# Hashed attention and a SiLU layer on one core: batch 0's second product in seven block products, shifted weight loads, and score products over all 128 rows

## The chip, the core and the metric

The kernel runs on one core of a Trainium2 chip. The core's engines run side by side, each through its own list of instructions in order: TensorE (PE in the profile; its weight loads are shown as PEld), VectorE (DVE), ScalarE (ACT), GpSimd (POOL) and SyncE (SP), which here only issues transfers. Transfers run on 16 DMA engines that all queues share. The metric is the device time of one execution in microseconds (us); the time before is the median of 11 runs, 300.68 us.

## The reference

Four batches of eight heads, 768 positions, head width 64. Queries and keys are hashed to six sign bits by a projection; a score counts only where all six bits of query and key agree. The attention output, 3072 tokens of width 512, goes through a layer with 2048 hidden units.

```python
q_bits = (einsum('bhsd,dk->bhsk', q, proj) > 0)
k_bits = (einsum('bhsd,dk->bhsk', k, proj) > 0)
mask   = (q_bucket[:, :, :, None] == k_bucket[:, :, None, :])
scores = where(mask, (1/8) * q @ k.T, -1e9)
attn   = softmax(scores)
x      = (attn @ v) rearranged to 3072 tokens x 512
h      = x @ w_in                      # 512 x 2048
out    = (h * sigmoid(h)) @ w_out      # 2048 x 512
```

## The kernel before

**Attention.** Heads go in pairs; pair p holds heads 2p and 2p+1 and there are 16 pairs, four to a batch. For each pair there is a tile `QKA` (even head) and a tile `QKB` (odd head), each 128 rows by 1536 columns of f16: q in the first 768 columns, k in the last. Four slots of each are used in turn (`p % NSL`). In `QKA` rows 0 to 63 hold the scaled head and the rows from 64 on hold the mask bits (six bits and a constant row), so that one product gives score plus mask; rows above 70 are not defined. In `QKB` rows 64 to 127 hold the head, the bits stand from row 0 on, and the rest of rows 0 to 63 was set to zero at the start (L159).

The work is cut into 288 units, nine to a head. Unit w has three parts: `score(w)` (L371), one or two matmuls with 512 columns in all into a PSUM tile `s_ps`, followed by ScalarE's exponential into `u`; and `av(w)` (L392), four matmuls of `u` with the values into `o_ps`. `score` runs three units ahead (`LEAD = 3`): loop turn w issues `av(w)` and then `score(w+3)`. The `s_ps` tiles have the tag "s" with three PSUM buffers, and the output tiles `o2_ps` of the hidden layer's second product have the same tag: while an output tile is open, the scores share the buffers that are left. Which buffer a tile gets is fixed when the program is built.

**How a pair gets ready.** Pairs from 6 on: `load_blocks(p)` (L86) brings q and k as eight transfers of 96 KB with 128-byte rows, issued by SP. `block_unit` (L252) transposes them on VectorE into `qk32`. `cast_unit` (L260, GpSimd) fills the head's rows. `proj_unit` (L282) multiplies `qk32` of two pairs with the projection on TensorE into two PSUM tiles of the tag "m" and VectorE makes bits of them. `bits_unit` (L334) puts the bits into `QKA` and `QKB`: by VectorE copies for pairs up to 7, and by eight small transfers on SP for each two pairs above 7 (L343).

**The hidden layer.** For each batch, `mm1` multiplies `w_in` with the transposed attention output `xT`, for 512 of the batch's tokens (ci 0, here called f) and for the other 256 (ci 1, here s), into `h_ps` (tag "m", three buffers). ScalarE takes the hyperbolic tangent and VectorE makes g of it (L492). The second product with `w_out` is done for batches 1 to 3, and for the last 256 tokens of batch 0, as a 2x2 block product with seven products instead of eight (`product`, L518): it needs sums of blocks of g (`comb`, L500) and combinations of blocks of `w_out` (`w_unit`, L181, on GpSimd, eight half steps of 128x1024). For the first 512 tokens of batch 0 it is done directly by `whole` (L554): four output tiles in turn, each with 16 matmuls of 512 columns in four parts, then one VectorE operation and a transfer out.

**Order.** `plan(w, fn)` hangs an operation on loop turn w (L665 to L724). The hidden layer's units stand in a queue `moeq`; at certain turns lists are added, and a running credit spreads them over the turns that remain until the next multiple of 72 (L732 to L758). Batch 0's first product and half of the second lie in turns 77 to 144 (`moe_list`, L613); what is left (`late`) lies between the first products of batch 1, from turn 145 on. All of TensorE's work is in one list, in this order.

**Names in the steps below.** L92: transfers of `load_blocks`. L177: the four loads of `w_out`, issued by GpSimd at turns 80, 84, 88, 92. L102: loads of v. L445: transposing transfer of `x_pr` to `xT`. L199 and L258: transposed q and k to `qk32`. L299: bits out of PSUM. L430: normalised attention output `x_pr`. L541 and L543: the ends of the seven products on ScalarE and VectorE.

Of the kernel before, what the change touches and what calls it, by code (L numbers as in the profile page):

```python
# [9 lines left out]
F32 = mybir.dt.float32  # L10
# [3 lines left out]
ALU = mybir.AluOpType  # L14
# [3 lines left out]
def kernel(  # L18
# [139 lines left out]
    for i in range(NSL):  # L158
        (nc.vector if i < 2 else nc.gpsimd).memset(QKB[i][0:64, :], 0.0)  # L159
    ident16 = cst.tile([P, P], F16, name="ident16")  # L160
# [160 lines left out]
    def bits_halves(p, par):  # L321
        t, r0 = ((QKA[p % NSL], 64), (QKB[p % NSL], 0))[par]
        for c in range(4):
            half, n = divmod(c, 2)
            x0 = n * S + half * HS
            r = slice(32 * c, 32 * c + NR)
            dst = t[r0 : r0 + NR, x0 : x0 + HS].rearrange("d (x c) -> d x c", c=P)
# [6 lines left out]
    def bits_unit(pairs, i, par):  # L334
# [12 lines left out]
        for n in range(2):  # L347
            c = 32 * (2 * i + n)
            r = slice(c, c + NR)
            dst = t[r0 : r0 + NR, n * S : (n + 1) * S].rearrange("d (x c) -> d x c", c=CB)  # L350
# [20 lines left out]
    def score(w):  # L371
# [3 lines left out]
        rows = slice(0, 65 + NBIT) if par == 0 else slice(0, P)  # L375
        sp = ps.tile([P, 512], F32, tag="s", name="s_ps", bufs=LEAD)
        for jt, c0, n, o0 in pts:
            nc.tensor.matmul(sp[:, o0 : o0 + n], t[rows, S + jt * P : S + (jt + 1) * P],  # L378
                             t[rows, c0 : c0 + n], start=True, stop=True)
# [76 lines left out]
    def moe_units(b):  # L456
# [43 lines left out]
        def comb(ci, n, f):  # L500
# [12 lines left out]
            eng = nc.gpsimd if n > 2 and scoring else nc.vector  # L513
# [40 lines left out]
        def whole(t, part):  # L554

            if part == 0:
                banks[t] = ps.tile([P, DMODEL], F32, tag="s", name="o2_ps", bufs=3)
            op = banks[t]
            for ft in range(4 * part, 4 * part + 4):
                x = blk[0, ft // NK][:, t // 2, ft % NK, t % 2 * P : (t % 2 + 1) * P]  # L560
                nc.tensor.matmul(op, x, w_out16[:, ft, :],  # L561
                                 start=(ft == 0), stop=(ft == NFT - 1))
            if part == 3:
                o = ops.tile([P, DMODEL], F32, tag="osb", name="osb", bufs=3)
                nc.vector.tensor_scalar(out=o, in0=op, scalar1=half_g, scalar2=None,
                                        op0=ALU.mult)
                dst = out[b * S : (b + 1) * S, :].rearrange("(p t) n -> p t n", p=P)
                nc.sync.dma_start(out=dst[:, t, :], in_=o)

# [11 lines left out]
        second[7] = then(second[7], (1, 1, al))  # L581
        if b == 0:
# [30 lines left out]
    def moe_list(b):  # L613
# [3 lines left out]
        if b == 0:  # L617
            units = first + spread(second, big[:8])
            late[:] = big[8:] + small
            return units  # L620
# [183 lines left out]
```

## Time and profile before

| what | us |
|---|---|
| median of 11 runs (lowest to highest) | 300.68 (298.76 to 303.47) |
| the profiled execution's own time | 299.74 |
| its span, first to last instruction | 298.0 |
| turns up to 76 (attention alone, plus six small units) | to 53.7 |
| turns 77 to 144 (batch 0's first product) | 53.7 to about 109.5 |
| the 72 turns after that | 109.5 to about 176 |
| end of the last score's exponential | about 240 |

The profile comes from one execution, so what follows is worked out against 299.74 us; the difference of 1.74 us to the span lies around the recorded instructions. Busy time of an engine is a union of its instructions. For TensorE it overstates how full the engine is, since a matmul's recorded length (379 ns with 512 columns, 272 ns with 256) includes the way through the array; successive matmuls start 0.22 us and 0.11 us apart. The page's second part shows the span in 40 slices of 7.45 us. The chain of waits goes back from the last instruction to what released each step. Groups of instructions end with the time that their engine was idle before them and with the releaser. A wait for several things is put down to the last one. Transfers are listed by queue: q1 is SP's, q0 is GpSimd's.

### The profile page before, as it was taken

The page shows a single profiled execution, that of the slowest core. Times are in us where ns is not written, and L with a number is a line of the kernel's source. Part 1 is how long each engine was busy: PE and PEld are TensorE (multiplying, and loading weights), DVE is VectorE, ACT ScalarE, POOL GpSimd, SP SyncE. Part 2 cuts the span into 40 slices and gives each one's busy share as a digit, 9 for nine tenths or more (in the row PEclk, how much of TensorE's full clock was granted, in tenths as well). Part 3 has the DMA queues.
Part 4 walks back from the last instruction along what each step waited for, and adds up shares of the span by engine and source line. Part 5 has one row for each costly group of instructions (what it writes and reads, how often), then busy time and mean ns, then how long its engine had stood idle before and what let it go on. Part 6 is the DMA issues. An engine that isn't in the chain of part 4 may idle for free.

```text
span 298.0 us, 7620 instructions
## 1 busy us (share of the span) xinstructions
PE 290.5 (98%) x2934; PEld 197.9 (66%) x2934; DVE 187.2 (63%) x362; ACT 217.1 (73%) x408; POOL 171.0 (57%) x223
## 2 busy tenths in 40 slices
PE   8999999999999989999999999999999999999995
PEld 3676755555666745567667888656668787667884
DVE  5797938899787364855798446954555453324262
ACT  5987989989987756877887786868888862446310
POOL 7589999388998644999257991599213730000000
PEclk9999999999999999999999999999999999999999
DMA  6999998999878919842299226103020113010113
GB/s 194 246 262 209 172 137 124 204 209 157 131 154 150 175 36 245 126 95 48 56 187 123 47 64 177 66 21 52 18 46 23 41 29 106 20 53 2 36 55 123
DMA packets 105716, 32.91 MB, mean 110 GB/s; under 512 B 90768, under 2 KB 105168, under 8 KB 105680
## 3 DMA queue, kind: packets, MB, share of 16 engines
q1 hardware_dynamic: 101296, 28.22, 45.9%
q0 software_dynamic: 4224, 4.19, 9.0%
q8 instruction: 23, 0.38, 0.6%
q14 instruction: 13, 0.11, 0.1%
q10 hardware_dynamic: 160, 0.00, 0.0%
HBM read 27.27 MB, written 6.29 MB: 113 GB/s over the span
## 4 chain that ended last, share of the span: by engine, by line
PE 95%; ACT 2%; DVE 1%; DMA 1%; issue 0%; SPq 0%; POOL 0%; ACTq 0%; POOLq 0%
PE h_ps L475 27%; PE o_ps L531 20%; PE s_ps L378 20%; PE o_ps L410 12%; PE o_ps L561 5%; PE bp_ps L293 3%; PE tp_ps L197 2%; ACT u L381 1%; PE warm_ps L125 1%; PE tp_ps L210 1%; DMA qka<-bits 1%; PE bp_ps L237 1%; DVE osb L543 1%; ACT th L489 0%; PE o_ps L401 0%
## 5 line engine op out<-in xcount | busy, mean ns | idle before, releaser
L381 ACT ACTIVATE u<-s_ps 128x512 f16<-128x512 f32 x288 | 156.9, 610 | 30.2 <-PE s_ps L378 29.6
L475 PE MATMUL h_ps<-xT,win 128*128 128x512 f16 (+1 forms) x512 | 98.4, 326 | 0.0
L410 PEld LDWEIGHTS <-u 128*128 128x128 f16 x1152 | 66.9, 98 | 38.1 <-ACT u L381 9.2
L410 PE MATMUL o_ps<-vv,u 128*128 128x65 f16 x1152 | 82.5, 194 | 0.6 <-ACT u L381 0.4
L492 DVE SCALAR_TENSOR_TENSOR g<-th,h_ps 128x512 f16<-128x512 f32 x72 | 48.5, 678 | 41.2 <-ACT th L489 40.9
L475 PEld LDWEIGHTS <-win 128*128 128x128 f16 x512 | 49.9, 98 | 24.9 <-issue 0.4
L378 PE MATMUL s_ps<-qka 71*128 71x512 f16 x192 | 52.9, 327 | 1.6 <-DMA qka<-bits 1.3
L531 PEld LDWEIGHTS <-g 128*128 128x128 f16 x480 | 46.8, 98 | 10.4 <-issue 1.1
L378 PE MATMUL s_ps<-qkb 128*128 128x512 f16 x192 | 52.9, 326 | 0.2 <-ACT u L381 0.2
L489 ACT ACTIVATE th<-h_ps 128x512 f32<-128x512 f32 x72 | 43.8, 608 | 11.3 <-PE h_ps L475 7.5
L430 POOL TENSOR_TENSOR x_pr<-osum,rec 128x384 f16<-128x384 f32 x23 | 19.7, 854 | 42.8 <-DVE rec L429 41.7
L543 DVE SCALAR_TENSOR_TENSOR osb<-o_ps,osb 128x256 f32<-128x256 f32 (+1 forms) x35 | 18.7, 535 | 22.8 <-PE o_ps L531 21.6
L263 POOL TENSOR_SCALAR qka<-qk 64x1536 f16<-64x1536 f32 x15 | 21.9, 1463 | 17.9 <-DVE qk L258 11.4
L531 PE MATMUL o_ps<-wt,g 128*128 128x256 f16 x240 | 30.7, 273 | 0.1
L531 PE MATMUL o_ps<-wout,g 128*128 128x256 f16 x240 | 30.4, 273 | 0.3 <-DVE osb L543 0.3
L485 ACT ACTIVATE g<-h_ps 128x512 f16<-128x512 f32 x24 | 14.3, 597 | 18.5 <-PE h_ps L475 18.5
L514 DVE TENSOR_TENSOR g<-g 128x1024 f16<-128x1024 f16 x24 | 18.2, 771 | 10.2 <-PE o_ps L531 5.3
L263 POOL TENSOR_SCALAR qkb<-qk 64x1536 f16<-64x1536 f32 x15 | 22.0, 1468 | 1.2
L274 POOL TENSOR_TENSOR vsa<-v_sb 128x192 f32<-128x192 f32 x32 | 18.9, 589 | 0.0
L272 POOL CAST vv<-v_sb 128x384 f16<-128x384 f32 x32 | 16.6, 520 | 1.0 <-DMA v_sb<-in_v_dram 0.6
L378 PEld LDWEIGHTS <-qka 71*128 71x128 f16 x192 | 15.5, 97 | 2.0 <-POOL vs L277 1.4
L561 PE MATMUL o_ps<-wout,g 128*128 128x512 f16 x64 | 16.4, 379 | 0.3 <-ACT u L381 0.2
(84 smaller groups left out, 295.7 us busy)
## 6 DMA issues: line engine op xcount, KB each, us to landing
v_sb<-in_v_dram SPq DMA_DIRECT2D x15, 384.0 KB
out_dram<-osb SPq DMA_DIRECT2D x16, 256.0 KB
q_blk<-in_q_dram SPq DMA_DIRECT2D x40, 96.0 KB
k_blk<-in_k_dram SPq DMA_DIRECT2D x40, 96.0 KB
win<-in_moe_w_in_dram POOLq DMA_DIRECT2D x4, 512.0 KB, 6.3
wout<-in_moe_w_out_dram POOLq DMA_DIRECT2D x4, 512.0 KB, 7.5
out_dram<-osb SPq DMA_DIRECT2D x16, 128.0 KB
q_sb<-in_q_dram SPq DMA_DIRECT2D x5, 384.0 KB
```

What stands on the lines that cost most here:

```text
L263: nc.gpsimd.tensor_scalar(out=dst[rows, :], in0=qk32[p][rows, :], scalar1=CS, scalar2=1.0, op0=ALU.mult, op1=ALU.mult)
L274: nc.gpsimd.tensor_tensor(out=sa, in0=src[:, 0:3], in1=src[:, 3:6], op=ALU.add)
L378: nc.tensor.matmul(sp[:, o0 : o0 + n], t[rows, S + jt * P : S + (jt + 1) * P], t[rows, c0 : c0 + n], start=True, stop=True)
L381: nc.scalar.activation(out=u, in_=sp, func=AF.Exp, scale=ESC)
L410: nc.tensor.matmul(o_ps[h][:, c0 // P + i, :], u[:, o0 + i * P : o0 + (i + 1) * P], vv[:, jt, :], start=(not direct(h) and w % NU == 0 and ...
L430: (nc.vector if direct(h) else nc.gpsimd).tensor_tensor(out=x_pr[p][:, :, par * D : (par + 1) * D], in0=o[:, 0:NJ, 0:D], in1=rec[:, :, Non ...
L475: nc.tensor.matmul(hp[:, :, j, :], w_in16[:, dt, ft * P : (ft + 1) * P], xT[4 * b + dt][:, c0 : c0 + n] .rearrange("d (r c) -> d r c", r=2 ...
L489: nc.scalar.activation(out=th, in_=hp, func=AF.Tanh, scale=0.5)
L492: nc.vector.scalar_tensor_tensor(out=g, in0=th.rearrange("p r f c -> p r (f c)"), scalar=1.0, in1=hp.rearrange("p r f c -> p r (f c)"), op ...
L531: nc.tensor.matmul(op[:, t, :], x[:, k, t * P : (t + 1) * P], y[:, k], start=(first and k == 0), stop=True, skip_group_check=True)
L543: nc.vector.scalar_tensor_tensor(out=o, in0=op, scalar=half_g, in1=kept[ci, add], op0=ALU.mult, op1=ALU.add)
L561: nc.tensor.matmul(op, x, w_out16[:, ft, :], start=(ft == 0), stop=(ft == NFT - 1))
```

## The change

It has five parts.

1. Batch 0's first 512 tokens go through `product` too: seven products in two halves of eight matmuls with 256 columns. `whole` is gone. The block sums that this needs (`comb` 1 to 4 in halves) are hung on batch 0's units and are all made by VectorE. Turns 77 to 144 get 30 units instead of 32, in the order "babababaaaaabb" (a: an s unit, b: a product half), and the late list takes products 5 and 3 of the large part with products 1 and 2 of the small part between them.
2. The last four half steps of `w_unit` stand at turns 145 to 148 instead of 146, 149, 157 and 160, with the third combination ahead of the fourth.
3. The loads of `w_out` stand at turns 88, 92, 96 and 100 instead of 80 to 92.
4. The block loads of pairs 10 and 11 stand at turns 121 and 130 instead of 116 and 117, so that on SP those of pair 11 come after the mask bits of pairs 8 and 9 (turn 128).
5. `score` uses all 128 rows of `QKA`. For that, rows 64 to 127 of the four tiles are set to zero at the start, one by VectorE, one by GpSimd and two by transfers on SP from the zeroed rows of `QKB`; and `QKA`'s bits are copied with 7 rows instead of 13.

```diff
--- before.py
+++ after.py
@@ -157,6 +157,10 @@
         nc.vector.memset(VS[i // 2][:, i % 2, D:E1], float(NJ))
     for i in range(NSL):
         (nc.vector if i < 2 else nc.gpsimd).memset(QKB[i][0:64, :], 0.0)
+    nc.vector.memset(QKA[0][64:128, :], 0.0)
+    nc.gpsimd.memset(QKA[1][64:128, :], 0.0)
+    for i in range(2, NSL):
+        nc.sync.dma_start(out=QKA[i][64:128, :], in_=QKB[i][0:64, :])
     ident16 = cst.tile([P, P], F16, name="ident16")
 
     w_in16 = cst.tile([P, NDT, DFF], F16, name="win")
@@ -323,8 +327,9 @@
         for c in range(4):
             half, n = divmod(c, 2)
             x0 = n * S + half * HS
-            r = slice(32 * c, 32 * c + NR)
-            dst = t[r0 : r0 + NR, x0 : x0 + HS].rearrange("d (x c) -> d x c", c=P)
+            nr = NR if par else NBIT + 1
+            r = slice(32 * c, 32 * c + nr)
+            dst = t[r0 : r0 + nr, x0 : x0 + HS].rearrange("d (x c) -> d x c", c=P)
             if n == 1 and par == 1:
                 nc.vector.tensor_scalar(out=dst, in0=bits[p][r, :, 0:P],
                                         scalar1=sc[r, 2:3], scalar2=None, op0=ALU.mult)
@@ -346,8 +351,9 @@
             return
         for n in range(2):
             c = 32 * (2 * i + n)
-            r = slice(c, c + NR)
-            dst = t[r0 : r0 + NR, n * S : (n + 1) * S].rearrange("d (x c) -> d x c", c=CB)
+            nr = NR if par else NBIT + 1
+            r = slice(c, c + nr)
+            dst = t[r0 : r0 + nr, n * S : (n + 1) * S].rearrange("d (x c) -> d x c", c=CB)
             if n == 1 and par == 1:
                 nc.vector.tensor_scalar(out=dst, in0=bits[pairs][r, :, 0:CB],
                                         scalar1=sc[r, 2:3], scalar2=None, op0=ALU.mult)
@@ -372,11 +378,10 @@
         h, pts = parts(w)
         p, par = divmod(h, 2)
         t = QKA[p % NSL] if par == 0 else QKB[p % NSL]
-        rows = slice(0, 65 + NBIT) if par == 0 else slice(0, P)
         sp = ps.tile([P, 512], F32, tag="s", name="s_ps", bufs=LEAD)
         for jt, c0, n, o0 in pts:
-            nc.tensor.matmul(sp[:, o0 : o0 + n], t[rows, S + jt * P : S + (jt + 1) * P],
-                             t[rows, c0 : c0 + n], start=True, stop=True)
+            nc.tensor.matmul(sp[:, o0 : o0 + n], t[:, S + jt * P : S + (jt + 1) * P],
+                             t[:, c0 : c0 + n], start=True, stop=True)
         u = upl.tile([P, 512], F16, tag="u", name="u")
         nc.scalar.activation(out=u, in_=sp, func=AF.Exp, scale=ESC)
         ut[w] = u
@@ -510,7 +515,7 @@
                              4: (a12, a12, a11, ALU.subtract)}[n]
             if n == 3:
                 dst = dst[:, f]
-            eng = nc.gpsimd if n > 2 and scoring else nc.vector
+            eng = nc.gpsimd if n > 2 and scoring and (b, ci) != (0, 0) else nc.vector
             eng.tensor_tensor(out=dst, in0=x, in1=y, op=op)
 
         banks, kept = {}, {}
@@ -551,22 +556,6 @@
                 "(p t) n -> p t n", p=P)
             nc.sync.dma_start(out=dst[:, t0 : t0 + nt, :], in_=o)
 
-        def whole(t, part):
-
-            if part == 0:
-                banks[t] = ps.tile([P, DMODEL], F32, tag="s", name="o2_ps", bufs=3)
-            op = banks[t]
-            for ft in range(4 * part, 4 * part + 4):
-                x = blk[0, ft // NK][:, t // 2, ft % NK, t % 2 * P : (t % 2 + 1) * P]
-                nc.tensor.matmul(op, x, w_out16[:, ft, :],
-                                 start=(ft == 0), stop=(ft == NFT - 1))
-            if part == 3:
-                o = ops.tile([P, DMODEL], F32, tag="osb", name="osb", bufs=3)
-                nc.vector.tensor_scalar(out=o, in0=op, scalar1=half_g, scalar2=None,
-                                        op0=ALU.mult)
-                dst = out[b * S : (b + 1) * S, :].rearrange("(p t) n -> p t n", p=P)
-                nc.sync.dma_start(out=dst[:, t, :], in_=o)
-
         def then(fn, *combs):
 
             def unit():
@@ -579,11 +568,14 @@
         first = [lambda grp=grp: mm1(0, grp) for grp in range(NFT)]
         second = [lambda grp=grp: mm1(1, grp) for grp in range(NFT // 2)]
         second[7] = then(second[7], (1, 1, al))
+        big = [lambda n=n, t=t: product(0, n, t)
+               for n in (1, 2, 6, 5, 3, 7, 4) for t in range(2)]
         if b == 0:
-            big = [lambda t=t, part=part: whole(t, part) for t in range(4) for part in range(4)]
+            for grp, c in ((3, (0, 1, lo)), (4, (0, 1, hi)), (5, (0, 2, lo)), (6, (0, 2, hi))):
+                second[grp] = then(second[grp], c)
+            for i, c in ((4, (0, 4, lo)), (5, (0, 4, hi)), (6, (0, 3, lo)), (7, (0, 3, hi))):
+                big[i] = then(big[i], c)
         else:
-            big = [lambda n=n, t=t: product(0, n, t)
-                   for n in (1, 2, 6, 5, 3, 7, 4) for t in range(2)]
             first[13] = then(first[13], (0, 1, lo))
             for grp, c in ((0, (0, 1, hi)), (1, (0, 2, hi)), (3, (0, 4, lo)), (4, (0, 3, lo))):
                 second[grp] = then(second[grp], c)
@@ -615,13 +607,16 @@
 
         first, second, big, small = moe_units(b) if b else first_units
         if b == 0:
-            units = first + spread(second, big[:8])
-            late[:] = big[8:] + small
-            return units
-        units = spread(first[:-3], late) + [big[0]] + first[-3:] + [big[1]]
-        for i, c in enumerate("ababaababababa"):
-            units.append((second, big)["ab".index(c)][("ababaababababa"[:i].count(c)) + 2 * (c == "b")])
+            units, order = first, "babababaaaaabb"
+        else:
+            units = spread(first[:-3], late) + [big[0]] + first[-3:] + [big[1]]
+            order = "ababaababababa"
+        n = order.count("b")
+        mixed = {"a": deque(second), "b": deque(big[:n] if b == 0 else big[8 - n : 8])}
+        units += [mixed[c].popleft() for c in order]
         late[:] = big[8:] + small
+        if b == 0:
+            late[:] = big[6:8] + small[:1] + big[8:10] + small[1:2] + big[10:] + small[2:]
         return units
 
 
@@ -688,7 +683,7 @@
         plan(21 + i, lambda p=4 + i: load_qk(p))
     for i in range(4):
         plan((24, 40, 68, 74)[i], lambda i=i: load_w_in(i))
-        plan(80 + 4 * i, lambda i=i: load_w_out(i))
+        plan(88 + 4 * i, lambda i=i: load_w_out(i))
 
     for i in range(6):
         plan(QST - 3 + 3 * i, lambda i=i: t_unit(4 + i // 3, i % 3))
@@ -714,10 +709,10 @@
             for j in range(2):
                 plan(w0 + 18 + 9 * i + 2 * j, lambda p=2 * Q + i, j=j: v_unit(p, (j,)))
             if Q + 1 < NQUAD:
-                plan(w0 + (28 if Q == 3 else 8) + i, lambda p=2 * Q + 2 + i: load_blocks(p))
+                plan(w0 + {3: 28, 4: 13 + 9 * i}.get(Q, 8) + i, lambda p=2 * Q + 2 + i: load_blocks(p))
     for i, n in enumerate((1, 2, 4, 3)):
         for half in range(2):
-            plan((104, 107, 110, 112, 146, 149, 157, 160)[2 * i + half],
+            plan((104, 107, 110, 112, 147, 148, 145, 146)[2 * i + half],
                  lambda n=n, half=half: w_unit(n, half))
     for p in range(NPAIR):
         plan((30, 42, 58, 75)[p] if p < 4 else 2 * NU * (p + 1) + (2 if p % 4 == 3 else 9),
```

## The prediction

> **What bounds the kernel now.** I read the page's busy shares first, then its slices, then the sums by stage, and last the timeline and the DMA queues around the changed turns.
>
> ```profile
> PE 290.5 (98%) x2934; PEld 197.9 (66%) x2934; DVE 187.2 (63%) x362; ACT 217.1 (73%) x408; POOL 171.0 (57%) x223
> PE   8999999999999989999999999999999999999995
> DMA  6999998999878919842299226103020113010113
> 53.70:109.50 55.80, 53.63 (x549) 33.08 (x549) 42.58 (x72) 47.67 (x93) 41.39 (x55) 1.00 0.90 157
> ```
>
> TensorE is full nearly everywhere, so work taken off it shortens the run, and a hole in it lengthens it. Two things qualify this. In turns 77 to 144 (last line; the columns are PE, PEld, DVE, ACT, POOL, clock, DMA share, GB/s) ScalarE is busy for 47.67 of 55.80 us, and the DMA engines are 90% busy. That is where the change works.
>
> The holes of TensorE in these turns are of two kinds. One is the wait for mask bits, late on SP's queue; the other is the wait for a score buffer:
>
> ```profile
> 88.62 0.28 PE L410 MATMUL o_ps<-vv,u 128*128 128x65 f16 x4
> 89.19 0.38 PE L378 MATMUL s_ps<-qka 71*128 71x512 f16 x1 [0.29 <-ACT u L381]
> ...
> 104.61 0.28 PE L410 MATMUL o_ps<-vv,u 128*128 128x65 f16 x4
> 106.17 0.38 PE L378 MATMUL s_ps<-qka 71*128 71x512 f16 x1 [1.27 <-DMA qka<-bits]
> ...
> 108.78 1.02 PE L561 MATMUL o_ps<-wout,g 128*128 128x512 f16 x4 [0.21 <-ACT u L381]
> ```
>
> Four `av` matmuls need 0.12 us start to start, so the next matmul is late by 0.45, 1.44 and (against 108.19 + 0.22) 0.37 us.
>
> How long a score buffer stays taken shows where nothing else is in the way, at the first score:
>
> ```profile
> 8.06 0.81 PE L378 MATMUL s_ps<-qka 71*128 71x512 f16 x4
> 8.48 1.08 ACT L381 ACTIVATE u<-s_ps 128x512 f16<-128x512 f32 x2 [0.25 <-PE s_ps L378]
> 9.12 0.17 PEld L410 LDWEIGHTS <-u 128*128 128x128 f16 x4 [0.53 <-ACT u L381]
> ```
>
> From the score's start to the moment at which its exponential lets TensorE go on, 9.12 - 8.06 = 1.06 us pass. A turn without a hidden-layer unit is 0.22 + 0.12 = 0.34 us of TensorE, one with a unit 0.34 + 0.87 = 1.21 us. With three buffers nobody waits; with two, the second bare turn in a row waits 1.06 - 2 x 0.34 = 0.38 us (measured above: 0.45); with one, each bare turn waits 0.72 us.
>
> Last, a transfer that is just in time now, and what GpSimd's queue does to SP's:
>
> ```profile
> 89.58 1.59 DVE L258 STREAM_TRANSPOSE qk<-k_blk 128x768 f32<-128x768 f32 x1 [0.19 <-DMA k_blk<-in_k_dram]
> ...
> 92.60 1.50 PE L293 MATMUL bp_ps<-qk,pw 128*32 128x512 f32 x16
> ...
> q0 software_dynamic: 336, 0.34, 118.7%
> q1 hardware_dynamic: 45, 0.01, 3.6%
> ```
>
> The last k block of pair 9 lands at 89.58, its transpose ends at 91.17, and 1.43 us later TensorE runs turn 128's projection, which needs it. The two queue lines are the DMA view for 73 to 75 us: while a load of `w_out` (q0) moves 0.34 MB, the block transfers (q1) move 0.01 MB.
>
> **What the Trainium skill says.** "TensorE: Matmul & The Clock Gate", section "LDWEIGHTS (loading the stationary operand)": a weight load's time follows its columns, not the rows of the contraction. The trace agrees: 97 ns on average with 71 rows and with 128. "DMA: Bandwidth & Descriptors", section "Queues, rings and completion order": each DMA engine takes turns between queues a packet (a group of descriptors) at a time, not a byte at a time. A queue of 128-byte rows then gets few bytes beside one of 1 KB rows. The trace agrees (0.01 beside 0.34 MB here, 0.05 beside 0.34 MB at 43 to 45 us).
>
> **The change part by part** (minus is gain).
>
> Seven products. In the chain of waits a part of `whole` has 0.87 us (four matmuls with 512 columns), eight matmuls with 256 columns 0.87 to 0.88. 16 x 0.865 = 13.84 becomes 14 x 0.875 = 12.25: -1.6 us, all on TensorE. ScalarE gets two more ends of products at 597 ns (the 128x512 row of L541) in the stage where it is 85% busy: between 0 and +1.2 us, I take +0.4. VectorE gets five ends at 690 ns for four at 679 and eight sums at 0.68 to 0.77, about 6.7 us in all, spread over turns 113 to 168, where it is busy about two thirds; between 0 and +1, taken at 0. The sums at turns 130 to 138 are its densest place.
>
> Rows. Weight loads are equal, but in the trace's start times the matmul after a 71-row one comes 220 ns later instead of 216 (512 columns) and 113 instead of 109 (first of two with 256). That is 13 ns in three turns of an even head; in the 114 even turns from 60 on 0.5 us. Before that ScalarE sets the pace, and it is worth nothing. Taken: -0.5, bounds 0 and -0.7. At the start VectorE's extra fill (698 ns like L159's) follows at 4.02 and ends at 4.72, before its next work at 4.99. GpSimd's (1369 ns) ends at 5.45 and pushes v's preparation from 6.58 to 7.30; its next copy ran at 7.33. SP's two fills (0.4 MB) delay the loads behind them by about 1.3 us; pair 2's q, the first of these, has that much before turn 12. All taken at 0, at most +0.5.
>
> Mask bits. On SP the bits now follow pair 10's loads, and pair 11's come after. SP spent 95.59 to 101.01 issuing pair 11's blocks, with the bits at 103.13. They come some 5 us earlier relative to the rest: -1.3 (the wait as the page counts it), the cover being anything up to 1.4.
>
> Score buffers. Which tile takes which buffer is known from the built programs. The old waits in this stretch go: 0.45 + 0.13 + 0.37 + 0.27 (at 114.55) = -1.2. New ones: with one output tile open, second bare turns are the ones that issue scores 118, 129 and 147: 3 x 0.38. From turn 148 the late list opens the small part's tile while the large part's second is open, and scores 151 to 155 stand in one single buffer; turns 149 and 151 are bare: 2 x 0.72. Scores 174 to 177 stand in one buffer again, and turn 172 is bare: 0.72. Together +3.3; ScalarE's other work can add to it, and a turn that is late anyway takes some away (2 to 4.5).
>
> `w_unit` earlier: 4 x 2.12 us on GpSimd from about 110 to 118.5, before products 7 (turn 157, about 120) need them; the normalisation at turn 152 and pair 10's casts queue behind and have over 10 us. 0.
>
> Loads of `w_out`. GpSimd reaches them in its own order. The first took 0.76 us at 52.49; now it follows pair 7's casts, at 66.3. The others follow the pieces of v's preparation around them, at about 69.7, 72.3 and 75.7. Data begins about 2 us after the issue and a load takes 3 us (0.52 MB at about 0.17 MB/us). So from 68.5 to 81 q0 moves four loads, where two were moved before. SP's queue issues pair 8's and 9's blocks from 69.33, held before that by pair 4's transposing transfer, so it can't use the calm from 58 to 66. Two more loads are 6 us in which the blocks get about 0.02 MB/us rather than 0.10: 0.47 MB less, caught up at 0.13 MB/us (0.91 MB in 80 to 87): the blocks land 3.6 us later (2.5 to 5). Behind the waiting transpose on VectorE stand a g, a normalisation and the bits; on TensorE the projection of turn 128 waits, and everything behind it. Transposed at 91.17 + 3.6 = 94.8. TensorE would be there at 92.60 - 0.87 (one unit fewer by then) - 0.45 + 0.76 (scores 118, 129) = 92.04: +2.7 us (1.6 to 4.1). Below 0.9 us of delay it costs nothing.
>
> Sum: -1.6 + 0.4 - 0.5 - 1.3 - 1.2 + 3.3 + 2.7 = +1.8. Against the profiled execution 299.74 + 1.8 = 301.5; the median shown is 0.94 above that execution, so 302.5.
>
> **Rivals.**
> A, the forecast: +1.8, own range +0.3 to +4.
> B, the other side, not slower: the block loads keep pace, because queues share better than at 73 to 75 us. Place: turn 128's projection; price 2.7; it decides as soon as the delay is under 0.9 us. Then 300.68 - 0.9 = 299.8. For it: during 68.5 to 72 us q1 still moved 0.14 MB beside 0.49. Against: three other loads show q1 nearly stopped.
> C: B, and the single-buffer turns cost nothing new either, as the waits move the later turns to where ScalarE is free: 300.68 - 4.2 = 296.5. For it: one-buffer waits are only worked out, the two-buffer kind alone was seen. Against: 0.45 measured where 0.38 was worked out.
> D: A, and the bits don't come in time either, since SP's loads of pair 10 are late by the same 3.6 us, or VectorE stays behind with its new sums: 1.3 to 2 more, 304.2. For it: SP and VectorE are in order. Against: by then the scores are later too.
>
> **How the numbers follow.** A 52%, B 17%, C 13%, D 18%. The predicted time is A's, 302.5. A change of 0.5%, 1.5 us, is about what a measurement of this kernel can tell from none. Slower by more: D and 72% of A, 0.55. Faster by more: C and 30% of B, 0.18. Within: 0.27. The range leaves out C and the far end of D: 298.8 to 305.5.
>
> **What would show it.** Right: VectorE's transposes of pairs 8 and 9 wait for `q_blk` or `k_blk` by some us around 88 to 93, TensorE's projection L293 has a hole before it there, q0 is dense from 68 to 81; in turns 149, 151 and 172 the score waits about 0.7 us for `u`; no wait for `qka<-bits` is left; the matmuls' sum falls by 1.6. Wrong: no wait at L258 and the projection on time (B), or no such waits of scores (C). A hole in the first 20 us would mean that the fills cost something.

## The result: 303.23 us, 1.0% more than before

The changed kernel takes 303.23 us (median of 12 executions, 302.26 to 306.81); the kernel before took 300.43 us in the same comparison (47 executions). The ratio is 1.0103, with a 95% interval of 1.0077 to 1.0128, or about 3 us more; it is taken over the executions in the core's faster state, and so isn't quite the quotient of the two medians (1.0093). The profiled execution's span is 301.0 us, against 298.0 before.

The busy shares and two rows of slices on the page of the changed kernel:

```profile
PE 290.4 (96%) x2982; PEld 202.9 (67%) x2982; DVE 197.2 (66%) x372; ACT 217.8 (72%) x410; POOL 175.9 (58%) x224
PE   8999999989999998999999999999999999999995
DMA  6999988939989549962088535201010213010113
```

TensorE is as busy as before (290.4 us against 290.5) in a longer span. The fall of 1.6 us that the prediction named as a mark doesn't show here: a score counts as busy for 0.38 us where the next matmul follows 0.22 us after its start, so a part of every short wait counts as busy. Its waits, from the view of waits (total, times, longest):

```profile
PE s_ps L383 <- ACT u L386: 2.8, 7, 0.6
PE bp_ps L297 <- DVE g L497: 1.3, 2, 0.8
...
PE bp_ps L297 <- DVE qk L262: 0.4, 1, 0.4
```

Of the seven waits of a score for its buffer one, at score 283, stands in the kernel before too, which had two of this kind (0.5 us) and one for mask bits (1.3 us); so six are new. The projection waits three times; before it did not. These figures count only the time in which no matmul is recorded. Below, a wait is counted from the trace's start times, as in the prediction: how much later a matmul starts than the one before it allows (0.22 us behind 512 columns, 0.12 us behind four `av` matmuls). Counted so, the six are 0.39 to 0.79 us long, and a seventh new one of 0.30 us, at score 156, comes to light.

To see where the time goes, the starts of the exponentials of equal scores are set against each other, after minus before, in us.

| score | 90 | 98 | 118 | 130 | 134 | 142 | 146 | 154 | 174 | 178 | 286 |
|---|---|---|---|---|---|---|---|---|---|---|---|
| difference | 0.0 | +1.5 | 0.0 | +1.1 | +2.7 | +1.8 | +0.3 | +2.0 | +2.1 | +2.8 | +2.7 |

Nothing is lost in the first 60 us. Time goes at scores 94 to 98 (63 to 67 us), 126 to 134 (90 to 97 us), 150 to 154 (112 to 116 us) and 174 to 178 (137 us); it is won at 98 to 118, where in the end two units of the hidden layer fewer have run ahead of a score (one of them is made up by score 128), and at 142 to 146, where the mask bits were waited for. VectorE's transposes of the first two places, and behind the first a g, from the timeline:

```profile
62.55 1.58 DVE L262 STREAM_TRANSPOSE qk<-k_blk 128x768 f32<-128x768 f32 x1 [1.49 <-DMA k_blk<-in_k_dram]
63.98 0.67 DVE L497 SCALAR_TENSOR_TENSOR g<-th,h_ps 128x512 f16<-128x512 f32 x1
...
83.94 1.63 DVE L262 STREAM_TRANSPOSE qk<-q_blk 128x768 f32<-128x768 f32 x1 [1.68 <-DMA q_blk<-in_q_dram]
...
90.22 1.62 DVE L262 STREAM_TRANSPOSE qk<-q_blk 128x768 f32<-128x768 f32 x1 [1.45 <-DMA q_blk<-in_q_dram]
...
93.44 1.63 DVE L262 STREAM_TRANSPOSE qk<-k_blk 128x768 f32<-128x768 f32 x1 [1.08 <-DMA k_blk<-in_k_dram]
```

The last one stood at 89.58 before. It ends at 95.07; the prediction had 94.8. The first one, for pair 7 at 62.55, no step of the prediction had; in the kernel before it waits for nothing:

```profile
61.62 1.53 DVE L258 STREAM_TRANSPOSE qk<-k_blk 128x768 f32<-128x768 f32 x1
```

TensorE's projections at both places in the changed kernel:

```profile
64.70 1.06 PE L297 MATMUL bp_ps<-qk,pw 128*32 128x512 f32 x8 [0.81 <-DVE g L497]
66.23 0.64 PE L297 MATMUL bp_ps<-qk,pw 128*32 128x256 f32 x8 [0.46 <-DVE g L497]
...
93.70 1.06 PE L297 MATMUL bp_ps<-qk,pw 128*32 128x512 f32 x6
95.12 1.48 PE L297 MATMUL bp_ps<-qk,pw 128*32 128x512 f32 x10 [0.36 <-DVE qk L262]
96.53 0.30 PE L415 MATMUL o_ps<-vv,u 128*128 128x65 f16 x4
```

In the kernel before, turn 128's projection takes 1.43 us from its first matmul (92.60) to the next matmul behind it (94.03). Here it takes 2.83 us, so TensorE loses 1.4 us at this place. That is more than the 0.36 us in brackets, since the last ten matmuls alone take 1.48 us, nearly as long as all 16 together did (1.50 us). At the first place the loss, with the waiting ahead of the projection, is 1.5 us.

At 64.70 the wait is put down to g. But g stands on VectorE's queue behind the transpose that waited for its block: the PSUM tile that the projection wants is freed by that g, so by the order on VectorE it is the late k block of pair 7 that is waited for. How the blocks at 90 us became late shows on SP's queue, where the issue of pair 8's k block was held up (5.88 us before):

```profile
70.33 4.10 SPq L92 DMA_DIRECT2D q_blk<-in_q_dram  x4
74.53 9.71 SPq L92 DMA_DIRECT2D k_blk<-in_k_dram  x4
```

The score waits foreseen at turns 149 and 151 (scores 152 and 154) are there. The first, four `av` matmuls (0.12 us) after 113.34, was due at 113.46:

```profile
113.34 0.28 PE L415 MATMUL o_ps<-vv,u 128*128 128x65 f16 x4
114.24 0.38 PE L383 MATMUL s_ps<-qka 128*128 128x512 f16 x1 [0.62 <-ACT u L386]
```

It starts 0.79 us late by the trace's unrounded times; the second, due at 115.79, 0.72 us late.

### The profile page after: what moved, and what is told of

Its sections match the earlier page's. It is cut to its first block, busy times and chain, and to the rows that moved or that the text cites. A ratio compares the mean times of both kernels' runs of the same rounds, so it can differ in the third digit from the quotient of the medians.

```text
span 301.0 us, 7740 instructions
## 1 busy us (share of the span) xinstructions
PE 290.4 (96%) x2982; PEld 202.9 (67%) x2982; DVE 197.2 (66%) x372; ACT 217.8 (72%) x410; POOL 175.9 (58%) x224
## 4 chain that ended last, share of the span: by engine, by line
PE 81%; DVE 6%; DMA 4%; SPq 4%; ACT 2%; issue 1%; POOL 0%; DVEq 0%; ACTq 0%; POOLq 0%
PE h_ps L480 23%; PE o_ps L536 22%; PE s_ps L383 16%; PE o_ps L415 10%; DMA k_blk<-in_k_dram 4%; SPq L92 4%; PE bp_ps L297 3%; PE tp_ps L201 2%; DVE qk L262 2%; DVE g L519 1%; PE warm_ps L125 1%; ACT u L386 1%; DVE g L497 1%; DVE osb L548 1%; PE tp_ps L214 1%
## 5 line engine op out<-in xcount | busy, mean ns | idle before, releaser
L536 PEld LDWEIGHTS <-g 128*128 128x128 f16 x576 | 56.1, 98 | 14.2 <-issue 2.7
L383 PE MATMUL s_ps<-qka 128*128 128x512 f16 x192 | 52.7, 326 | 1.4 <-ACT u L386 1.3
L548 DVE SCALAR_TENSOR_TENSOR osb<-o_ps,osb 128x512 f32<-128x512 f32 (+1 forms) x40 | 22.2, 554 | 23.5 <-PE o_ps L536 22.2
L536 PE MATMUL o_ps<-wt,g 128*128 128x256 f16 x288 | 37.1, 273 | 0.3 <-DVE g L519 0.2
L536 PE MATMUL o_ps<-wout,g 128*128 128x256 f16 x288 | 36.7, 273 | 0.3 <-DVE osb L548 0.3
L519 DVE TENSOR_TENSOR g<-g 128x1024 f16<-128x1024 f16 x30 | 25.4, 859 | 9.4 <-ACT g L490 4.7
L262 DVE STREAM_TRANSPOSE qk<-q_blk 128x768 f32<-128x768 f32 x10 | 15.9, 1589 | 3.1 <-DMA q_blk<-in_q_dram 3.1
L262 DVE STREAM_TRANSPOSE qk<-k_blk 128x768 f32<-128x768 f32 x10 | 16.0, 1595 | 2.7 <-DMA k_blk<-in_k_dram 2.6
```

Source lines behind the costliest of these rows:

```text
L262: nc.vector.transpose(out=dst, in_=qk_sb[p, "qk"[n]])
L383: nc.tensor.matmul(sp[:, o0 : o0 + n], t[:, S + jt * P : S + (jt + 1) * P], t[:, c0 : c0 + n], start=True, stop=True)
L519: eng.tensor_tensor(out=dst, in0=x, in1=y, op=op)
L536: nc.tensor.matmul(op[:, t, :], x[:, k, t * P : (t + 1) * P], y[:, k], start=(first and k == 0), stop=True, skip_group_check=True)
L548: nc.vector.scalar_tensor_tensor(out=o, in0=op, scalar=half_g, in1=kept[ci, add], op0=ALU.mult, op1=ALU.add)
```

## The experiments

Twelve kernels were run. Each was timed in five rounds beside the kernel before. Each heading says which kernel the edit is made to; the labels a1 to a4 are edits to the changed kernel. Where a kernel is compared with the changed one, the ratios to the kernel before are subtracted and taken times 300 us; the two intervals together leave about 1 us open in such a difference. Where two profiles are compared at a score, what they differ in by score 90 (up to 0.7 us) is taken off. What a projection loses is counted as above, against a projection for which nothing is late.

**a1_wout80: the loads of `w_out` where they were.**

```diff
-        plan(88 + 4 * i, lambda i=i: load_w_out(i))
+        plan(80 + 4 * i, lambda i=i: load_w_out(i))
```

> The changed kernel with the loads of w_out back at turns 80, 84, 88, 92 (changed: 88 to 100). Theory (late loads of w_out starve pair 8's and 9's blocks): the transposes of pairs 8 and 9 no longer wait for q_blk or k_blk by more than 0.3 us, the hole ahead of turn 128's projection goes, and the time falls by about 1.5 to 2 us against the changed kernel (ratio to before about 1.004). The hole of 1.8 us at 63 to 66 us stays (it is put down to the fills) or grows by up to 0.5, since a load of w_out is at work there again. Rival (waits only move, ScalarE at 85% is the bound in turns 77 to 144): the hole goes, but the next score-buffer waits grow by as much and the time falls by less than 0.5 us.

Measured: ratio 1.0035 (1.0004 to 1.0066), 2.0 us less than the changed kernel. The last transpose in its timeline, and the projection, now without a hole:

```profile
89.68 1.60 DVE L262 STREAM_TRANSPOSE qk<-k_blk 128x768 f32<-128x768 f32 x1 [0.68 <-DMA k_blk<-in_k_dram]
```

```profile
92.61 1.50 PE L297 MATMUL bp_ps<-qk,pw 128*32 128x512 f32 x16
```

The rival falls: the score waits behind it stay as they were (0.45, 0.79, 0.72, 0.32, 0.72 us) and don't grow. VectorE still waits 0.68 us for this block, which should have been 0.3 at most, but TensorE no longer does. The other half of the expectation failed: the hole at 63 us, which should have stayed, is not there, though the fills on SP's queue are.

**a2_memset: the fills of `QKA[2]` and `QKA[3]` without SP.**

```diff
-    for i in range(2, NSL):
-        nc.sync.dma_start(out=QKA[i][64:128, :], in_=QKB[i][0:64, :])
...
+    for i in range(2, NSL):
+        plan(i, lambda i=i: nc.gpsimd.memset(QKA[i][64:128, :], 0.0))
```

> The changed kernel with the zero fills of QKA[2] and QKA[3] done by GpSimd at turns 2 and 3 instead of by two transfers on SP's queue. Theory (0.39 MB of fills push SP's whole chain, so pair 7's last k block falls under a load of w_in): the transpose of k_blk at 62 us starts about 1 us earlier, without a wait over 0.3 us, and the two waits of TensorE at 64.7 and 66.2 us (0.97 and 0.84 us late) go; 0.7 to 1.5 us less than the changed kernel, most of it kept to the end. Rival (fills are hidden, as the prediction took it; the hole is from chance in one execution or from another transfer): the hole stays and the time is the same within 0.3 us.

Measured: 1.0066 (1.0043 to 1.0089), 1.1 us less than the changed kernel; no hole at 63 us. As expected, but taken with a1 it doesn't settle the matter, because there the hole went with the fills in place.

**a3_late: one output tile at a time.**

```diff
-            late[:] = big[6:8] + small[:1] + big[8:10] + small[1:2] + big[10:] + small[2:]
+            late[:] = big[6:10] + small[:2] + big[10:] + small[2:]
```

> The changed kernel with the late products in another order: big's tile is finished before a tile of the small part is opened (late list big 6 to 9, small 0 and 1, then the rest), so that never two of the three buffers are held at once. Theory (double holding costs 0.79, 0.72, 0.30 and 0.72 us at the scores 152, 154, 156 and 175): these waits of 0.7 us go, of the second bare turns behind a single open tile some 0.4 us each stay, and the time falls by 1 to 2 us against the changed kernel. Rival (ScalarE sets the pace there anyway): the waits spread over other turns and the time falls by less than 0.5 us.

Measured: 1.0081 (1.0053 to 1.0109), 0.7 us less than the changed kernel, under what was expected and within the noise. The waits of scores 152, 154, 156 and 175 (2.5 us) go. But three others come: a product that adds into its tile waits until the product before it has been read out (0.61 us between products 5 and 3, 0.30 us between the small part's first two), and the small part's tile waits 0.89 us for a buffer. Together 1.8 us, which leaves 0.7. This kernel has no edit ahead of 100 us, but in its profile no hole at 63 us comes first; its projection of turn 128:

```profile
92.11 1.06 PE L297 MATMUL bp_ps<-qk,pw 128*32 128x512 f32 x6
94.98 1.48 PE L297 MATMUL bp_ps<-qk,pw 128*32 128x512 f32 x10 [1.82 <-DVE qk L262]
96.39 0.30 PE L415 MATMUL o_ps<-vv,u 128*128 128x65 f16 x4
```

It loses 2.9 us, against 1.4 in the profile of the changed kernel, which lost 1.5 at 63 us. At score 142 both kernels are behind the kernel before by nearly the same, 1.7 and 1.8 us. So against a3 the hole at 63 us cost nothing more in the end: TensorE would have waited for a block of this date at 95 us anyway. The date itself isn't firm: with the same loads of `w_out`, the last transpose ends at 95.07 (changed), 94.93 (a3) and 93.98 us (a2), and a2 loses only 1.4 us here. Whether that is due to the fills or to chance isn't shown.

**a4_all: the three edits together.**

The edit is the three diffs above in one kernel.

> The three edits together. Theory: the three costs lie at different places (63 to 66, 91 to 95, 112 to 138 us) and add, 4 to 5 us less than the changed kernel, which is 1 to 2.5 us faster than the kernel before (ratio 0.992 to 0.997). Rival (waits only move): under 1.5 us less than the changed kernel, ratio 1.005 or more.

Measured: 298.88 us, ratio 0.9959 (0.9939 to 0.9979): 4.3 us less than the changed kernel, where the three alone sum to 3.8. Within the noise the costs add, and this version is faster than the kernel before.

**b1_rows: the kernel before with the fills and the 128 rows alone.**

```diff
+    nc.vector.memset(QKA[0][64:128, :], 0.0)
+    nc.gpsimd.memset(QKA[1][64:128, :], 0.0)
+    for i in range(2, NSL):
+        nc.sync.dma_start(out=QKA[i][64:128, :], in_=QKB[i][0:64, :])
...
-        rows = slice(0, 65 + NBIT) if par == 0 else slice(0, P)
...
-            nc.tensor.matmul(sp[:, o0 : o0 + n], t[rows, S + jt * P : S + (jt + 1) * P],
-                             t[rows, c0 : c0 + n], start=True, stop=True)
+            nc.tensor.matmul(sp[:, o0 : o0 + n], t[:, S + jt * P : S + (jt + 1) * P],
+                             t[:, c0 : c0 + n], start=True, stop=True)
```

> The kernel before with one part of the change alone: scores over 128 rows, with the zero fills that it needs (two of them transfers on SP's queue). Theory (fills are hidden; the hole at 63 us in the changed kernel's profile came and went with the sharing of the DMA engines, since two kernels with the same fills don't show it): 0.2 to 0.5 us less than before, ratio 0.998 to 1.000, no hole at 63 to 66 us, pair 7's k block transposed without a wait over 0.3 us. Rival (fills cost 1 us or more, as the run with fills on GpSimd suggests): ratio 1.002 to 1.005.

Measured: 1.0018 (0.9984 to 1.0051), between both expectations, and the interval excludes neither. The executions spread from 298.56 to 307.80 us, and the profiled one is among the long ones (305.59; the median is 301.84). In it the hole is there, and larger:

```profile
64.45 1.55 DVE L262 STREAM_TRANSPOSE qk<-k_blk 128x768 f32<-128x768 f32 x1 [2.75 <-DMA k_blk<-in_k_dram]
```

**b4_fills: a4 with the fills on SP's queue again.**

The edit is the diffs of a1 and a3 in the changed kernel.

> The changed kernel with the loads of w_out at turns 80 to 92 and the late products in the other order, but with the fills on SP's queue as the change has them (it differs from the run with all three edits by the place of the fills alone). Theory (fills are hidden): the same time as that run within 0.6 us, ratio 0.994 to 0.998. Rival (fills on SP cost 1 us): ratio 0.999 to 1.001.

Measured: 0.9976 (0.9948 to 1.0004), 0.5 us over a4; the intervals overlap. Its profiled execution, again above the median (301.35 against 299.51), has the hole too:

```profile
63.57 1.55 DVE L262 STREAM_TRANSPOSE qk<-k_blk 128x768 f32<-128x768 f32 x1 [2.30 <-DMA k_blk<-in_k_dram]
```

Over all profiles: with the two transfers on SP, TensorE loses 1.5 us or more at 63 us in three of six (the changed kernel, b1, b4; not a1, a3, c4); without them in none of eight (c1 loses 0.5 us there). The block bytes (128-byte packets) that have arrived in the traces by 56 us, when `w_in`'s last loads have the engines, go with it: 1.33, 1.38 and 1.43 of 1.57 MB with the hole, 1.48 to 1.57 MB in all others. A reading that fits is a backlog: in the page's slices the DMA engines are at least 90% busy from 7.5 to 37.6 us, and 0.39 MB of fills then still stand in front of pair 6's and 7's blocks, which start to move after 37 us. With the fills 0 to 0.24 MB of these had come by 40 us, without them 0.18 to 0.39. These ranges overlap, and the way from the fills to the late block isn't shown step by step. So theory and rival were both half right: the hole comes in some executions and not in others, far from the place where the fills are issued, and over 1 us only with the fills on SP. A count of executions in the last section points the same way. Three comparisons of medians (a2, b4, and b1 against the 0.3 us that the rows give) say 0.5 to 1 us; only a2's is beyond its interval, and barely.

**b2_wout88: the kernel before with the later loads of `w_out` alone.**

```diff
-        plan(80 + 4 * i, lambda i=i: load_w_out(i))
+        plan(88 + 4 * i, lambda i=i: load_w_out(i))
```

> The kernel before with the loads of w_out planned at turns 88 to 100 instead of 80 to 92, and nothing else. Theory: the last k block of pair 9 is transposed at about 95.0 us instead of 91.17, the fourth matmul of turn 128's projection waits 1.5 to 2.2 us, the wait for mask bits at 104.7 us stays between 1 and 2.5 us since SP's queue is late as a whole; 1.6 to 3.5 us more than before, ratio 1.005 to 1.012. Rival (block loads keep pace): same time, ratio within 0.998 to 1.002.

Measured: 1.0116 (1.0061 to 1.0171), 3.5 us more; the rival falls. The last transpose:

```profile
95.11 1.53 DVE L258 STREAM_TRANSPOSE qk<-k_blk 128x768 f32<-128x768 f32 x1 [2.12 <-DMA k_blk<-in_k_dram]
```

TensorE stands idle for 2.60 us in the projection, and the bits are waited for as before (1.65 us). But at score 134 this profile is 5.7 us behind, over twice that. The rest shows in the view by stretches (PE, PEld, DVE, ACT, POOL busy, then the granted clock, DMA share, GB/s):

```profile
94.00:96.00 2.00, 0.10 (x1) 0.00 (x0) 0.89 (x1) 0.00 (x0) 0.00 (x0) 1.00 1.07 356
...
97.00:98.00 1.00, 1.00 (x9) 0.29 (x2) 0.86 (x3) 0.00 (x0) 1.00 (x1) 0.74 1.05 110
98.00:99.00 1.00, 1.00 (x7) 0.34 (x6) 1.00 (x3) 0.00 (x0) 0.92 (x2) 0.50 0.30 23
99.00:100.00 1.00, 1.00 (x9) 0.45 (x7) 0.93 (x2) 0.47 (x1) 0.92 (x2) 0.50 0.66 104
100.00:102.00 2.00, 2.00 (x18) 1.53 (x17) 0.00 (x0) 1.25 (x4) 1.92 (x4) 0.78 0.86 135
```

After the hole TensorE ran at half its clock for some 3.4 us.

**c4_blocks: the changed kernel with pair 8's and 9's blocks earlier.**

```diff
-                plan(w0 + {3: 28, 4: 13 + 9 * i}.get(Q, 8) + i, lambda p=2 * Q + 2 + i: load_blocks(p))
+                plan(w0 + {3: 20, 4: 13 + 9 * i}.get(Q, 8) + i, lambda p=2 * Q + 2 + i: load_blocks(p))
```

> The changed kernel with the block loads of pairs 8 and 9 eight turns earlier (planned at 92 and 93 instead of 100 and 101), ahead of pair 4's transposing transfer on SP's queue; loads of w_out stay at 88 to 100. Theory (the loss at turn 128 is the sharing of DMA engines with the late w_out loads, not the place of those loads as such): the blocks land before 75 us in the calm stretch, no wait at their transposes, no hole at the projection of turn 128, 1.5 to 2 us less than the changed kernel, ratio 1.002 to 1.005. Rival (SP's queue as a whole is late, or the loads then fall under w_in and w_out at once): the hole stays, or pair 7's k block is late and TensorE waits at 63 us; ratio 1.008 or more.

Measured: 1.0020 (0.9999 to 1.0041), 2.5 us less than the changed kernel with `w_out` as late as there. SP issues the blocks from 53 us:

```profile
53.09 9.76 SPq L92 DMA_DIRECT2D q_blk<-in_q_dram  x4
...
71.74 7.20 SPq L92 DMA_DIRECT2D k_blk<-in_k_dram  x4
79.03 3.43 SPq L450 DMA_TRANSPOSE xT<-x_pr  x1
```

No transpose waits, and the projection has no hole:

```profile
92.33 1.50 PE L297 MATMUL bp_ps<-qk,pw 128*32 128x512 f32 x16
```

The blocks landed later than expected (issued up to 78.9 us instead of landing by 75), so they still met `w_out` on the DMA engines. But they had a head start, and the late loads as such cost nothing.

**b3_bits: the kernel before with pairs 10's and 11's loads as changed, alone.**

```diff
-                plan(w0 + (28 if Q == 3 else 8) + i, lambda p=2 * Q + 2 + i: load_blocks(p))
+                plan(w0 + {3: 28, 4: 13 + 9 * i}.get(Q, 8) + i, lambda p=2 * Q + 2 + i: load_blocks(p))
```

> The kernel before with the loads of pairs 10 and 11 at turns 109 and 119 beyond the stage's start offset as in the changed kernel (13 and 23 turns into it), so that the mask bits of pairs 8 and 9 go ahead of pair 11's blocks, and nothing else. Theory: the wait of 1.44 us for qka<-bits at 104.7 us goes, nothing takes its place; 1.2 to 1.5 us less, ratio 0.995 to 0.996. Rival (a wait only moves): ScalarE or a score buffer holds the next turns, or pair 11's blocks come late at turn 152; less than 0.5 us gained.

(Pair 11's loads stand at turn 131 in this kernel and in the changed one, not at 130 as the description of the change has it.)

Measured: 298.49 us, ratio 0.9945 (0.9922 to 0.9967). SP issues the bits at 97.89 us instead of 103.13; the wait goes, a wait of 0.55 us for a score buffer, before 107.88, takes the place of one of 0.37, and at score 286 the profile is 1.39 us ahead. The rival falls.

**c1_seven: the kernel before with the seven products alone.**

```diff
-            big = [lambda t=t, part=part: whole(t, part) for t in range(4) for part in range(4)]
+            for grp, c in ((3, (0, 1, lo)), (4, (0, 1, hi)), (5, (0, 2, lo)), (6, (0, 2, hi))):
+                second[grp] = then(second[grp], c)
+            for i, c in ((4, (0, 4, lo)), (5, (0, 4, hi)), (6, (0, 3, lo)), (7, (0, 3, hi))):
+                big[i] = then(big[i], c)
...
+            late[:] = big[6:8] + small[:1] + big[8:10] + small[1:2] + big[10:] + small[2:]
...
-            plan((104, 107, 110, 112, 146, 149, 157, 160)[2 * i + half],
+            plan((104, 107, 110, 112, 147, 148, 145, 146)[2 * i + half],
```

> The kernel before with the seven products for batch 0 alone (with their order, sums, and w_unit at 145 to 148; loads, fills and rows as before). Theory: 1.5 us less of TensorE and 1.2 us of old score-buffer waits gone, 3.9 us of new ones (the seven of the changed kernel's profile), and the wait for mask bits at about 104 us, which are no earlier, takes 1.4 to 2.6 us (1.4 before); together 1 to 2.5 us more than before, ratio 1.003 to 1.008. Rival (the products gain, and all of the loss is in the loads and fills): 0.5 us or more less than before, ratio at most 0.998.

Measured: 1.0033 (1.0007 to 1.0058), 1.0 us more. Its profile is that of the fastest of its 22 executions (299.12 us; the median is 301.10): there the bits happen to be issued at 100.47 and aren't waited for, and six score waits (0.39, 0.53, 0.44, 0.79, 0.72 and 0.27 us) make 3.1 us. For the median the loss is shown; that it is the bits' wait again is argued from the expectation alone, as no profile of a median execution exists.

**c2_bits_rows: the kernel before with bits and rows, fills by GpSimd.**

The edit is b3's diff and b1's, the latter with the two transfers replaced as in a2.

> The kernel before with mask bits ahead of pair 11's blocks and scores over 128 rows, the fills of QKA[2] and QKA[3] by GpSimd. Theory: 1.4 us from the bits and 0.3 us from the rows (0.14 us were seen to go in the last 100 turns of the changed kernel), 1.7 us less than before, ratio 0.993 to 0.995; from score 186 to 286 the matmuls gain 0.14 us on the kernel before. Rival (rows are worth nothing, or GpSimd's fills delay the start): ratio 0.9945 or more, as with the bits alone.

Measured: 298.35 us, ratio 0.9940 (0.9914 to 0.9967). At score 286 it is 1.68 us ahead of the kernel before, where b3 is 1.39 ahead; from score 186 to 286 it gains 0.14. By these two profiles the rows are worth 0.3 us. By ratio it can't be told from b3 and a4; all three beat both kernels. It has no seven products, and a4, which adds them and has no late loads, is 1.31 us ahead at score 286: even there the products win nothing.

**c3_order: a4 with units between the products that add to the same tile.**

```diff
-            units, order = first, "babababaaaaabb"
+            units, order = first, "babababaaaabb"
...
-            late[:] = big[6:10] + small[:2] + big[10:] + small[2:]
+            late[:] = big[6:8] + second[7:] + big[8:10] + small[:2] + big[10:] + [lambda: None] + small[2:]
```

> The run with all three edits, with the last hidden-layer unit of the second group moved between products 5 and 3 of batch 0, small 0 as last unit of the head, small 1 behind it with other units between, and an empty unit ahead of small 2. Theory (a product that adds to a buffer waits for the read of the product before it: 0.61 us between products 5 and 3, 0.30 us between small 0 and 1): these two waits go, the opening of small's tile (0.87 us) stays; 0.5 to 1 us less than that run, ratio 0.9925 to 0.9945. Rival (the order only moves the waits): the same as that run, ratio 0.995 to 0.997.

Measured: 1.0015 (0.9994 to 1.0035), 1.7 us more than a4. The two waits went, and others came that are longer; the order of the sums and of VectorE's reads moved with the units:

```profile
102.23 0.61 PE L534 MATMUL o_ps<-wt,g 128*128 128x256 f16 x4 [0.34 <-DVE g L517]
103.69 0.50 PE L534 MATMUL o_ps<-wt,g 128*128 128x256 f16 x3 [0.85 <-DVE g L517]
...
116.69 0.38 PE L381 MATMUL s_ps<-qkb 128*128 128x512 f16 x1 [1.27 <-DVE osb L546]
```

Here product 6 comes before its sum is done, and a score waits for the read of the tile whose buffer it gets. The rival was right, and too mild.

## Why the prediction was right, step by step

The forecast was A, slower by 1.8 us; measured are 3.1 by the ratio, 2.7 at score 286 of the profile.

| step | predicted | measured | from |
|---|---|---|---|
| seven products | -1.6 | -1.5 | a4's profile: -1.31 at score 286, less -1.44 (bits), -1.22 (old waits), -0.31 (rows), +3.15 (its own waits) |
| two more product ends | +0.4 | no wait of their own | part of the buffer waits |
| rows | -0.5 | -0.3 | c2 against b3 |
| fills | 0 | +0.5 to +1 | medians of a2, b1, b4; 1.5 in the changed kernel's profile |
| mask bits | -1.3 | -1.4 | b3's profile; 0.0055 x 300 = 1.65 by its ratio |
| old buffer waits | -1.2 | -1.2 | gone in the profile |
| new buffer waits | +3.3 | +3.9 | seven new waits in the profile |
| `w_out` loads | +2.7 | +2.0 to +2.5 | a1, c4; 2.9 in a3's profile, 1.4 in the changed kernel's |

The measured terms sum to about 2.5 us with the middle of each range. In the changed kernel's own profile the sum closes: -1.6 (fewer columns), -0.3, -1.4, -1.2, +3.9, +1.5 (the hole at 63 us), +1.4 (turn 128) and +0.4 (a product that waits for its sum, see below) are +2.7, as at score 286. So the forecast came near partly by luck: in this profile the term of `w_out` is 1.3 us smaller than forecast, while the hole put down to the fills, which were taken at nothing, is 1.5.

**`w_out` loads.** Right in place, chain and date: late by 3.86 us at the last transpose where 3.6 was worked out. The Trainium skill's statement on turns between queues ("DMA: Bandwidth & Descriptors", "Queues, rings and completion order") carried this step. It gave the direction, not the share: in the trace, from 76 to 84 us q1 moved 0.48 MB in 128-byte packets beside 1.16 MB of q0, about 0.06 MB/us, and 0.14 MB/us from 88 to 92 us with q0 silent. The prediction's 0.02 was too low, but the sharing lasted longer than its 6 us: by 84 us 0.59 MB of blocks had come where the kernel before had 1.10, 0.51 MB less for the 0.47 worked out. Two errors cancel here; its 0.13 for the catching up fitted. GpSimd issued the four loads 1 us later than worked out (67.24 to 76.66), because its casts waited for the k block that was late at 63 us. The loss at turn 128 is 1.4 us in this profile, and not 2.7, since TensorE came there 1.7 us later than worked out (93.70 for 92.04); a3 shows the full size, 2.9.

**Score buffers.** All six places were right (0.39, 0.53 and 0.45 for three of 0.38; 0.79, 0.72 and 0.72 for three of 0.72). They stand at the scores that it named: 118, 129 and 147, and 152, 154 and 175, issued in turns 149, 151 and 172. The seventh, 0.30 us at score 156 where the small part's tile is still held, was not foreseen, and ScalarE's other work lengthened the two-buffer waits a little: together the missing 0.6 us.

**Fills: the step that failed.** "All taken at 0, at most +0.5" looked for the first load that could be late and stopped at pair 2's q. The right question was when the DMA engines would next have room for 0.4 MB. In the page's slices they were at least 90% busy until 37.6 us, and the load that then came late, pair 7's k block, was due over 50 us after the fills. The runs show the place and, with the noise said above, the size; that a backlog carries the delay there is the reading that fits.

**VectorE's sums.** Taken at 0; product 6 waited once for its sum, 0.39 us before 105.87, in the kernels with the late projection (the changed one, a2, a3), not in a1 and a4. It is a part of rival D, though too small to be it. B and C fell: blocks don't keep pace, and the one-buffer waits are there.

## What to carry to other kernels

A saving in matrix columns counts only after subtracting what holds a PSUM buffer longer: fourteen half products were 1.5 us shorter than sixteen parts, and waited 2 to 3 us more for buffers (1.2 us before; 3.1 and 3.9 us in a4 and the changed kernel). The parts of the change that paid are the smallest ones, the order on SP's queue and the rows. An added transfer is to be followed to the next stretch in which the DMA engines have room, not to the next transfer on its queue; and where two queues with rows of 1 KB and of 128 bytes meet, as here, a head start for the small rows takes the cost away (c4). Two waits for transfers with a fixed date don't add up, the later takes in the earlier (1.5 and 1.4 us in the changed kernel, 2.9 at once in a3), while the waits for buffers here do.

## What the runs showed that was not expected

TensorE's clock can fall after a single hole. In b2, after two matmuls 3.19 us apart from start to start (the trace shows 2.60 us of idle), and in b1 at a wait for mask bits (2.95 us from start to start, 2.75 us of it shown as idle), the clock went to 0.50 and stayed there for about 3.4 us: matmuls of 512 columns came 408 to 427 ns apart instead of 215. Holes of 2.4 us from start to start (a3) and less left it at 1.00. The Trainium skill ("TensorE: Matmul & The Clock Gate", "Part 1: The HAM clock gate (the "warmup" mystery)") says that the array goes to half its clock after an idle window of about 3.4 us and needs as long a busy window to come back. The trace agrees with the second half; for the first, 2.95 and 3.19 us from start to start were enough. 3.4 us at half clock lose another 1.7 us on top of the wait.

A fall shows in an execution's mean granted clock, without a profile: 3.4 us at half clock in 298 give 0.994. Of the kernel before, 39 of the 177 executions timed beside the experiments had a mean of 0.995 or less; of b3 and c2, where the bits are ahead, none of 41. It fits a wait for the bits that is at times twice as long as the profiled 1.44 us; no profile of such an execution of the kernel before was taken, so this isn't shown.

The bits can't be all of it. Of the kernels that have them ahead and the fills on SP (the changed one, a1, a3, b4, c4), 12 of 88 executions show such a mean; of those that have them ahead and no fills on SP (a2, a4, b3, c2, c3), 1 of 90. That is the strongest sign that the fills cost time in some executions; where in these executions the clock fell isn't known.
